# Two decode-attention layers on one core: key and value loads in 16 KB pieces, wq spread over all partitions

## Chip, cores and metric

One Trainium2 chip, one core of it, the other cores idle. The metric is the device time of one execution in microseconds. Every kernel but one was run several times. Where a ratio is given, it is the mean time of one kernel's fast runs over that of the other's fast runs of the same rounds on the same chip, so it is not quite the ratio of the medians that stand beside it.

## The reference

Two independent single-token attention layers, A and B, with the same shapes. A sees only the last 2,048 cache rows, B all 8,192. Everything is bfloat16.

```
x: (1,1,576)   wq: (576, 32*128)   wo: (32*128, 576)   k_cache, v_cache: (1, 16, 8192, 128)
q = (x @ wq) as 32 heads of 128;  two query heads share one of 16 key/value heads
scores = q . k * 128**-0.5 over the window;  p = softmax(scores);  o = p . v
out = concat(o of all heads) @ wo;   A and B are concatenated
```

Nearly all the work is reading. A's keys and values are 16.8 MB, B's 67.1 MB, the two wq 9.4 MB and the two wo 9.4 MB, together 102.8 MB, and every byte is used once.

## The kernel before

A recorder gives every operation an engine and derives the semaphore waits. All large loads go out on one queue (SyncE) into a ring of twelve slots of 1 MB, 8 KB in each of 128 partitions. A slot is loaded again as soon as its last reader is done.

```python
SLOT = 4096; NSLOT = 12                     # bf16 elements per partition and slot; slots

def load_x(P):                              # x as one row
    act.dma_start(xrow[0:1, P * DM:(P + 1) * DM], xs[P][0, 0:1, :])

def load_wq(P, k):                          # five row tiles; the last has only 64 rows = 64 partitions
    rows = 128 if k < 4 else DM - 512
    return load(lambda: wqs[P][k * 128:k * 128 + rows, :], lambda v: v[0:rows, :], "wq")

def load_kv(arrs, P, c, i):                 # B: one head, 32 rows per partition, 8 KB in one run
    ...                                     # A: two heads, 16 rows per partition each, runs of 4 KB
    if HPS[P] == 1:
        return a[0, i, r0:r0 + n, :].rearrange("(p t) d -> p (t d)", p=128)
    return a[0, i * HPS[P]:(i + 1) * HPS[P], r0:r0 + n, :].rearrange("g (p t) d -> p g (t d)", p=128)
```

For each key slot TensorE makes 32 transposes of 128x128 into PSUM, ScalarE and VectorE copy them out, and 8 matmuls of 512 columns build the scores. Each value slot takes 32 matmuls. B's second pass over its keys is mixed with the values of the first, A's values with B's first keys. At the end come B's last 16 value slots and then B's wo, in pieces of 7, 7, 7, 7 and 4 rows per partition, so that the last piece is small.

## Time and profile before

| | before |
|---|---|
| time, median | 263.5 us (263.2 to 264.5) |
| bytes read | 102.8 MB |
| rate while B's 8 KB pieces stream | 420 GB/s |
| rate while A's 4 KB pieces stream | 409 GB/s |
| rate while a 64-row wq piece passes | 248 to 266 GB/s |
| packets on the load queue | 16,328 |

First the busy shares, the DMA rows and the packet count from the page of the kernel before. The two rows cut the span into 40 slices of 6.5 us: the busy share of the DMA engines in tenths, and what they moved.

```profile
PE 171.7 (66%) x3292; PEld 132.6 (51%) x3292; DVE 68.9 (26%) x126; ACT 85.2 (33%) x92; POOL 21.6 (8%) x31
...
DMA  7999999999999999999999999999999999999971
GB/s 263 420 328 409 409 417 419 233 421 414 418 414 410 421 413 414 416 420 416 424 420 419 419 420 421 419 420 420 421 422 415 425 421 419 422 417 421 423 325 55
DMA packets 16369, 103.22 MB, mean 396 GB/s; under 512 B 1618, under 2 KB 1620, under 8 KB 6996
```

The DMA engines are busy from the first load to the last, and no compute engine is above 66%. So a busy digit tells nothing more here; the rate does. Apart from both ends, two slices are low, the third (328) and the eighth (233), and the digit in both is still 9: the engines were occupied, but moved less.

The stretches view of the same kernel puts numbers on these places. After each stretch and its length come the busy times of the five engines, and at the end of the line the granted TensorE clock, the DMA share and the rate.

```profile
core 0: us, PE busy (x) PEld busy (x) DVE busy (x) ACT busy (x) POOL busy (x), PEclk, DMA share, GB/s
12.00:16.00 4.00, 1.04 (x8) 0.14 (x8) 0.00 (x0) 0.00 (x0) 4.00 (x1) 1.00 1.00 266
20.00:36.00 16.00, 15.85 (x238) 12.98 (x237) 8.30 (x12) 11.66 (x13) 2.79 (x9) 1.00 1.03 409
45.00:52.00 7.00, 1.66 (x16) 0.26 (x16) 0.00 (x0) 0.00 (x0) 0.00 (x0) 0.64 1.02 248
110.00:200.00 90.00, 64.94 (x1292) 52.28 (x1289) 31.28 (x53) 38.03 (x41) 0.00 (x0) 0.89 1.01 420
200.00:235.00 35.00, 16.26 (x484) 12.60 (x484) 0.76 (x4) 0.00 (x0) 0.00 (x0) 0.55 1.01 420
```

A missing 154 GB/s over 4 us and a missing 172 GB/s over 7 us, against 420, are 1.5 and 2.9 us of loading. Both stretches are those in which the 64-row tile of a wq passes.

The load queue's own waits, in total us, times, and longest:

```profile
SPq L105 <- PE ktps L335: 13.9, 11, 4.1
SPq L105 <- PE misc L483: 4.4, 4, 2.7
```

The queue (SP is SyncE, ktps the tile of transposed keys) sometimes has to wait for a slot, but none of these waits shows as a gap in the DMA row: twelve slots are far enough ahead.

Last, the end of the kernel, matmuls of wo in order of time (start, duration, instruction, and what was waited for):

```profile
256.08 1.03 PE L483 MATMUL misc<-slots,opj 128*32 128x144 bf16 x28 [1.84 <-DMA slots<-in_B_wo_dram]
257.48 0.67 PE L483 MATMUL misc<-slots,opj 128*32 128x144 bf16 x16 [0.36 <-DMA slots<-in_B_wo_dram]
```

Each piece is used as soon as it lands. What remains after the last landing is 0.7 us of matmuls, a copy and the store.

### The profile page before, as it was taken

The page shows a single profiled execution, that of the slowest core. Times are in us where ns is not written, and L with a number is a line of the kernel's source. Part 1 is how long each engine was busy: PE and PEld are TensorE (multiplying, and loading weights), DVE is VectorE, ACT ScalarE, POOL GpSimd, SP SyncE. Part 2 cuts the span into 40 slices and gives each one's busy share as a digit, 9 for nine tenths or more (in the row PEclk, how much of TensorE's full clock was granted, in tenths as well). Part 3 has the DMA queues.
Part 4 walks back from the last instruction along what each step waited for, and adds up shares of the span by engine and source line. Part 5 has one row for each costly group of instructions (what it writes and reads, how often), then busy time and mean ns, then how long its engine had stood idle before and what let it go on. Part 6 is the DMA issues. An engine that isn't in the chain of part 4 may idle for free.

```text
span 260.6 us, 7123 instructions
## 1 busy us (share of the span) xinstructions
PE 171.7 (66%) x3292; PEld 132.6 (51%) x3292; DVE 68.9 (26%) x126; ACT 85.2 (33%) x92; POOL 21.6 (8%) x31
## 2 busy tenths in 40 slices
PE   0559995179899795778967649768665443443472
PEld 0129781067687564748855438647553333232361
DVE  0014642026345242243633322232244000000000
ACT  2016872036377352445744324333340000000000
POOL 8994000000000000000000000000000000000000
PEclk9999999658799799797999997797886755555555
DMA  7999999999999999999999999999999999999971
GB/s 263 420 328 409 409 417 419 233 421 414 418 414 410 421 413 414 416 420 416 424 420 419 419 420 421 419 420 420 421 422 415 425 421 419 422 417 421 423 325 55
DMA packets 16369, 103.22 MB, mean 396 GB/s; under 512 B 1618, under 2 KB 1620, under 8 KB 6996
## 3 DMA queue, kind: packets, MB, share of 16 engines
q1 hardware_dynamic: 16328, 102.77, 97.4%
q8 instruction: 26, 0.43, 0.7%
q14 instruction: 3, 0.02, 0.0%
q10 hardware_dynamic: 12, 0.00, 0.0%
HBM read 102.76 MB, written 0.00 MB: 394 GB/s over the span
## 4 chain that ended last, share of the span: by engine, by line
DMA 56%; SPq 27%; PE 14%; issue 1%; DVE 1%; ACT 0%
SPq L244 27%; DMA slots<-in_B_v_cache_dram 21%; DMA slots<-in_B_k_cache_dram 10%; DMA slots<-in_B_wo_dram 10%; PE ktps L335 10%; DMA slots<-in_B_wq_dram 9%; DMA slots<-in_A_k_cache_dram 6%; PE sacc L356 2%; PE opsum L448 1%; PE misc L483 0%; DVE qrow L307 0%; PE opsum L298 0%; SPq L105 0%; PE misc L298 0%; DVE srow L411 0%
## 5 line engine op out<-in xcount | busy, mean ns | idle before, releaser
L335 PE MATMUL ktps<-ident,slots 128*128 128x128 bf16 x1280 | 94.0, 243 | 24.6 <-DMA slots<-in_B_k_cache_dram 24.2
L335 PEld LDWEIGHTS ktps<-ident,slots 128*128 128x128 bf16 x1280 | 87.6, 111 | 32.7 <-DMA slots<-in_B_k_cache_dram 28.4
L342 ACT ACTIVATE kt<-ktps 128x1024 bf16<-128x1024 bf16 x80 | 78.7, 1022 | 74.9 <-PE ktps L335 74.8
L345 DVE COPY kt<-ktps 128x1024 bf16<-128x1024 bf16 x80 | 55.4, 692 | 93.0 <-PE ktps L335 93.0
L448 PE MATMUL opsum<-slots,ptm 128*32 128x128 bf16 x1280 | 31.7, 256 | 26.6 <-DMA slots<-in_B_v_cache_dram 26.5
L448 PEld LDWEIGHTS opsum<-slots,ptm 128*32 128x32 bf16 x1280 | 24.5, 114 | 39.7 <-DMA slots<-in_B_v_cache_dram 35.1
L356 PE MATMUL sacc<-kt,qtm 128*32 128x512 bf16 x320 | 25.4, 395 | 0.7 <-DVE kt L345 0.7
L298 PE MATMUL opsum<-slots,xpad 128*32 128x512 bf16 (+1 forms) x40 | 5.6, 542 | 13.0 <-DMA slots<-in_B_wq_dram 7.9
L220 POOL MEMSET ptm<- 128x8192 uint32 x2 | 13.8, 6924 | 0.0
L483 PE MATMUL misc<-slots,opj 128*32 128x144 bf16 x256 | 8.4, 307 | 5.4 <-DMA slots<-in_B_wo_dram 3.3
L461 DVE TENSOR_SCALAR acc<-opsum,stat 128x128 f32<-128x128 f32 x2 | 0.7, 346 | 40.2 <-PE opsum L448 40.2
L298 PEld LDWEIGHTS opsum<-slots,xpad 128*32 128x32 bf16 (+1 forms) x40 | 1.2, 102 | 18.1 <-DMA slots<-in_B_wq_dram 9.9
L483 PEld LDWEIGHTS misc<-slots,opj 128*32 128x32 bf16 x256 | 6.6, 134 | 6.9 <-DMA slots<-in_B_wo_dram 4.2
L305 ACT ACTIVATE qrow<-opsum 128x512 bf16<-128x512 f32 x2 | 1.2, 597 | 25.8 <-PE misc L298 25.8
L356 PEld LDWEIGHTS sacc<-kt,qtm 128*32 128x32 bf16 x320 | 5.0, 95 | 5.9 <-ACT kt L342 1.6
L307 DVE CAST qrow<-misc 128x512 bf16<-128x512 f32 x2 | 1.4, 692 | 20.9 <-PE misc L298 20.9
L298 PE MATMUL misc<-slots,xpad 128*32 128x512 bf16 (+1 forms) x40 | 5.7, 557 | 0.0
L279 PE MATMUL misc<-onesb,xrow 1*128 1x1 bf16 (+1 forms) x10 | 0.8, 171 | 7.4 <-DMA xrow<-in_A_x_dram 7.4
L470 PE MATMUL misc<-acc,pick 128*128 128x32 f32 x16 | 3.5, 380 | 2.7 <-DVE acc L461 1.8
L376 ACT ACTIVATE psb<-sacc,stat 128x1024 bf16<-128x1024 f32 (+1 forms) x3 | 2.9, 971 | 6.8 <-DVE stat L374 6.8
L470 PEld LDWEIGHTS misc<-acc,pick 128*128 128x128 f32 x16 | 3.2, 300 | 3.5 <-DVE acc L461 2.3
L279 PEld LDWEIGHTS misc<-onesb,xrow 1*128 1x128 bf16 (+1 forms) x10 | 0.6, 100 | 7.9 <-DMA xrow<-in_A_x_dram 7.4
(52 smaller groups left out, 34.5 us busy)
## 6 DMA issues: line engine op xcount, KB each, us to landing
slots<-in_B_k_cache_dram SPq DMA_DIRECT2D x32, 1024.0 KB, 26.1
slots<-in_B_v_cache_dram SPq DMA_DIRECT2D x32, 1024.0 KB, 26.9
slots<-in_A_k_cache_dram SPq DMA_DIRECT2D x8, 1024.0 KB, 20.5
slots<-in_A_v_cache_dram SPq DMA_DIRECT2D x8, 1024.0 KB, 22.7
slots<-in_A_wq_dram SPq DMA_DIRECT2D x4, 1024.0 KB, 8.0
slots<-in_B_wq_dram SPq DMA_DIRECT2D x4, 1024.0 KB, 21.1
slots<-in_A_wo_dram SPq DMA_DIRECT2D x4, 1008.0 KB, 27.6
slots<-in_B_wo_dram SPq DMA_DIRECT2D x4, 1008.0 KB, 27.7
```

The source lines that it names most:

```text
L220: add("pool", lambda pool, b=b: pool.memset(ptm[:, b, :].bitcast(U32), 0), writes=[("ptm", b)])
L244: add("sp", lambda sp: sp.dma_start(view_of(slots[:, s, :]), src_of()), writes=[res], dma="slot%d" % s)
L279: ins = pe.matmul(misc[0:n, k:k + 1], lhsT=xrow[0:1, P * DM + k * 128:P * DM + k * 128 + n], rhs=onesb[0:1, 0:1], start=True, stop=True)
L298: ins = pe.matmul(qps[c][32 * j:32 * j + 32, :], lhsT=xpad[0:rows, P, k, :], rhs=slots[0:rows, s, n * 512:(n + 1) * 512], start=(k == 0), ...
L335: ins = pe.matmul(ktps_bf[q][:, t * 128:(t + 1) * 128], lhsT=slots[:, s, (8 * q + t) * 128:(8 * q + t + 1) * 128], rhs=ident[:, :], start= ...
L342: add("act", lambda act, q=q, dst=dst: act.activation(dst, ktps_bf[q], ACT.Copy), reads=[("bank", q)], writes=[("kt", u, q)])
L345: add("dve", lambda dve, q=q, dst=dst: dve.tensor_copy(dst, ktps_bf[q]), reads=[("bank", q)], writes=[("kt", u, q)])
L356: ins = pe.matmul(sacc[32 * j:32 * j + 32, h * 512:(h + 1) * 512], lhsT=qtm[:, P, g * 32:(g + 1) * 32], rhs=kt[:, u, o:o + 512], start=(g ...
L376: add("act", lambda act: act.activation(psb[:, pb, 0:w], sacc[:, 0:w], ACT.Exp, bias=st(P, C_NB + c), scale=SCALE, accum_out=st(P, C_L + c ...
L448: ins = pe.matmul(opsum[32 * j:32 * j + 32, 0:DH], lhsT=ptm[:, pb, o:o + 32], rhs=slots[:, s, t * 128:(t + 1) * 128], start=(g == 0 and b ...
L470: ins = pe.matmul(misc[:, 0:32], lhsT=pick[:, r, :], rhs=acc[:, d, 32 * r:32 * r + 32], start=(r == 0), stop=(r == 3))
L483: ins = pe.matmul(misc[32 * j:32 * j + 32, 0:OUTW], lhsT=opj[:, P, jj:jj + 32], rhs=slots[:, s, o:o + OUTW], start=(jj == 0), stop=(jj == ...
```

## The change

The intent is to have every large load move 16 KB per partition in one contiguous run, over all 128 partitions. Rows of a cache are 256 B, so 16 KB are 64 rows. One head's 2,048 or 4,096 rows then fill only 32 or 64 partitions, and the change fills the others with further heads: partition 4p+g (A) or 2p+g (B) holds rows of head g. wq is read as 64 x 2 runs of 36 KB, in pieces of 16, 16 and 4 KB; wo goes out in pieces of 15.75 and 4.5 KB.

```diff
-SLOT = 4096
-NSLOT = 12
-XT = 5
-WO_SLOT = 7
+SLOT = 8192
+UNIT = 4096
+NSLOT = 6
+TS = 64
+WQ_UNITS = 9
+WQ_SLOT = 4
+WO_SLOT = 14
@@ loads
-        rows = 128 if k < 4 else DM - 512
-        return load(lambda: wqs[P][k * 128:k * 128 + rows, :], lambda v: v[0:rows, :], "wq")
+        lo, hi = k * WQ_SLOT * 2048, min(WQ_UNITS, (k + 1) * WQ_SLOT) * 2048
+        return load(lambda: wqs[P].rearrange("(m r) n -> m (r n)", m=64)
+                    .rearrange("m (e y) -> (m e) y", e=2)[:, lo:hi],
+                    lambda v: v[:, 0:hi - lo], "wq")
-            if HPS[P] == 1:
-                return a[0, i, r0:r0 + n, :].rearrange("(p t) d -> p (t d)", p=128)
-            return a[0, i * HPS[P]:(i + 1) * HPS[P], r0:r0 + n, :].rearrange("g (p t) d -> p g (t d)", p=128)
+            return a[0, i * G[P]:(i + 1) * G[P], r0:r0 + CH[P], :].rearrange("g (p t) d -> p g (t d)", t=TS)
@@ x: one value per (row group, parity), multiplied by a parity mask, instead of a transposed row
+            add("dve", lambda dve, e=e: dve.tensor_scalar(xpad[:, P, 5 * e:5 * e + 5, 0], xtwo[:, P, 0:5],
+                                                          par[2][:, e:e + 1], None, ALU.mult), ...)
@@ scores: every second or fourth column of the transposed keys belongs to a head
-                                        lhsT=qtm[:, P, g * 32:(g + 1) * 32], rhs=kt[:, u, o:o + 512],
+                    rhs = kt[:, u, j * 1024:(j + 1) * 1024].rearrange("d (x g) -> d x g", g=G[P])[:, :, e]
@@ softmax: each probability is written once per interleaved head, then masked by partition
+            src = bass.AP(tensor=sacc, offset=0, ap=[[1024, 128], [1, w], [0, G[P]]])
+                    ins = dve.tensor_scalar(dst, src, par[G[P]][:, e:e + 1], None, ALU.mult)
... (value matmuls, schedule and output store follow the new slots: six of 2 MB)
```

The bytes and the number of key transposes and value matmuls stay the same. About half as many load instructions go out (52 instead of 100).

More of the change, by code (lines that the diff above doesn't have):

```diff
@@ L155, in bass_concat_heads__sliding_block_cached__gqa_block_cached__decode_kernel @@
     base = [SK - W_A, 0]
-    CH = [W_A, SLOT]
-    HPS = [SLOT // CH[P] for P in range(2)]
+    G = [4, 2]
+    PH = [128 // G[P] for P in range(2)]
+    CH = [TS * PH[P] for P in range(2)]
     NCH = [S_len[P] // CH[P] for P in range(2)]
-    NT = [CH[P] // 128 for P in range(2)]
-    CB = [NT[P] // 4 for P in range(2)]
-    CW = [CB[P] * 128 for P in range(2)]
+    UW = [8 * PH[P] for P in range(2)]
+    CW = [2 * UW[P] for P in range(2)]
+    NS = [HKV // G[P] for P in range(2)]
     prog = Program(nc)
@@ L167, in bass_concat_heads__sliding_block_cached__gqa_block_cached__decode_kernel @@
     slots = nc.alloc_sbuf_tensor("slots", [128, NSLOT, SLOT], BF16)
-    kt = nc.alloc_sbuf_tensor("kt", [128, NKT, SLOT], BF16)
+    kt = nc.alloc_sbuf_tensor("kt", [128, NKT, UNIT], BF16)
     ptm = nc.alloc_sbuf_tensor("ptm", [128, 2, 32 * 512], BF16)
-    psb = nc.alloc_sbuf_tensor("psb", [128, 2, 1024], BF16)
+    psb = nc.alloc_sbuf_tensor("psb", [128, 2048], BF16)
     ident = nc.alloc_sbuf_tensor("ident", [128, 128], BF16)
@@ L175, in bass_concat_heads__sliding_block_cached__gqa_block_cached__decode_kernel @@
     selq = nc.alloc_sbuf_tensor("selq", [128, 4], BF16)
-    onesb = nc.alloc_sbuf_tensor("onesb", [128, 4], BF16)
     onesf = nc.alloc_sbuf_tensor("onesf", [128, 4], F32)
     qtm = nc.alloc_sbuf_tensor("qtm", [128, 2, HKV * 32], BF16)
-    xrow = nc.alloc_sbuf_tensor("xrow", [1, 2 * DM], BF16)
-    xpad = nc.alloc_sbuf_tensor("xpad", [128, 2, XT, 32], BF16)
+    xtwo = nc.alloc_sbuf_tensor("xtwo", [128, 2, 8], BF16)
+    xpad = nc.alloc_sbuf_tensor("xpad", [128, 2, 10, 32], BF16)
+    par = [None, None, nc.alloc_sbuf_tensor("par2", [128, 2], F32), None, nc.alloc_sbuf_tensor("par4", [128, 4], F32)]
     qrow = nc.alloc_sbuf_tensor("qrow", [128, 1024], BF16)
@@ L205, in setup @@
         zero(selq[:])
-        pool.memset(onesb[:], 1.0)
         pool.memset(onesf[:], 1.0)
@@ L209, in setup @@
         return zero(qtm[:])
-    add("pool", setup, writes=["ident", "xpad", "selq", "ones", "warm", ("qtm", 0), ("qtm", 1)])
+    add("pool", setup, writes=["ident", ("xpad", 0), ("xpad", 1), "selq", "ones", "warm", ("qtm", 0), ("qtm", 1)])
     def select(t, base_, pattern, mult):
@@ L233, in bass_concat_heads__sliding_block_cached__gqa_block_cached__decode_kernel @@
         add("pool", select(same[:], 32 * dj, [[-1, 128]], 1), reads=["same"], writes=["same"])
+    for n in (2, 4):
+        add("dve", lambda dve, n=n: dve.tensor_reduce(par[n][:, :], ident[:, :].rearrange("p (m g) -> p g m", g=n),
+                                                      AX.X, ALU.add),
+            reads=["ident"], writes=[("par", n)])
     add("act", lambda act: act.activation(warm[:, 4:8], warm[:, 0:4], ACT.Exp), reads=["warm"], writes=["warm2"])
@@ L247, in load_x, with go @@
     def load_x(P):
-        add("act", lambda act: act.dma_start(xrow[0:1, P * DM:(P + 1) * DM], xs[P][0, 0:1, :]),
-            writes=[("xrow", P)], dma="x%d" % P)
+        def go(act):
+            x = xs[P]
+            with nc.allow_non_contiguous_dma(reason="small x load"):
+                src = bass.AP(tensor=x.tensor, offset=x.offset, ap=[[9, 64], [4, 2], [1, 5]])
+                return act.dma_start(xtwo[:, P, 0:5], src)
+        add("act", go, writes=[("xtwo", P)], dma="x%d" % P)
     def load_wq(P, k):
-        rows = 128 if k < 4 else DM - 512
-        return load(lambda: wqs[P][k * 128:k * 128 + rows, :], lambda v: v[0:rows, :], "wq")
+        lo, hi = k * WQ_SLOT * 2048, min(WQ_UNITS, (k + 1) * WQ_SLOT) * 2048
+        return load(lambda: wqs[P].rearrange("(m r) n -> m (r n)", m=64)
+                    .rearrange("m (e y) -> (m e) y", e=2)[:, lo:hi],
+                    lambda v: v[:, 0:hi - lo], "wq")
     def load_kv(arrs, P, c, i):
-        n = CH[P]
-        r0 = base[P] + c * n
+        r0 = base[P] + c * CH[P]
         def src():
             a = arrs[P]
-            if HPS[P] == 1:
-                return a[0, i, r0:r0 + n, :].rearrange("(p t) d -> p (t d)", p=128)
-            return a[0, i * HPS[P]:(i + 1) * HPS[P], r0:r0 + n, :].rearrange("g (p t) d -> p g (t d)", p=128)
-        def view(v):
-            return v if HPS[P] == 1 else v.rearrange("p (g x) -> p g x", g=HPS[P])
-        return load(src, view, "kv")
+            return a[0, i * G[P]:(i + 1) * G[P], r0:r0 + CH[P], :].rearrange("g (p t) d -> p g (t d)", t=TS)
+        return load(src, lambda v: v, "kv")
     def load_wo(P, k):
@@ L275, in x_columns @@
     def x_columns(P):
-        def tr(pe):
-            for k in range(XT):
-                n = 128 if k < 4 else DM - 512
-                ins = pe.matmul(misc[0:n, k:k + 1], lhsT=xrow[0:1, P * DM + k * 128:P * DM + k * 128 + n],
-                                rhs=onesb[0:1, 0:1], start=True, stop=True)
-            return ins
-        add("pe", tr, reads=[("xrow", P), "ones"], writes=[B_M])
-        add("dve", lambda dve: dve.tensor_copy(xpad[:, P, 0:4, 0], misc[:, 0:4]),
-            reads=[B_M], writes=["xpad"])
-        add("dve", lambda dve: dve.tensor_copy(xpad[0:DM - 512, P, 4, 0:1], misc[0:DM - 512, 4:5]),
-            reads=[B_M], writes=["xpad"])
+        for e in range(2):
+            add("dve", lambda dve, e=e: dve.tensor_scalar(xpad[:, P, 5 * e:5 * e + 5, 0], xtwo[:, P, 0:5],
+                                                          par[2][:, e:e + 1], None, ALU.mult),
+                reads=[("xtwo", P), ("par", 2)], writes=[("xpad", P)])
     qps = [opsum, misc]
@@ L291, in q_part @@
     def q_part(P, k, s):
-        rows = 128 if k < 4 else DM - 512
         def mm(pe):
-            for c in range(2):
-                for j in range(4):
-                    n = 2 * j + c
-                    ins = pe.matmul(qps[c][32 * j:32 * j + 32, :], lhsT=xpad[0:rows, P, k, :],
-                                    rhs=slots[0:rows, s, n * 512:(n + 1) * 512],
-                                    start=(k == 0), stop=(k == XT - 1))
+            for u in range(k * WQ_SLOT, min(WQ_UNITS, (k + 1) * WQ_SLOT)):
+                for c in range(2):
+                    for j in range(4):
+                        n = 2 * j + c
+                        x = u // 2 if n // 4 == u % 2 else 5 + (u + 1) // 2
+                        o = (u - k * WQ_SLOT) * 2048 + (n % 4) * 512
+                        ins = pe.matmul(qps[c][32 * j:32 * j + 32, :], lhsT=xpad[:, P, x, :],
+                                        rhs=slots[:, s, o:o + 512], start=(u == 0), stop=(u == WQ_UNITS - 1))
             return ins
-        add("pe", mm, reads=["xpad", ("slot", s)], writes=qbank)
+        add("pe", mm, reads=[("xpad", P), ("slot", s)], writes=qbank)
     def q_finish(P):
@@ L327, in bass_concat_heads__sliding_block_cached__gqa_block_cached__decode_kernel, with k_transpose @@
     k_count = [0]
-    def k_transpose(s):
+    def k_transpose(s, half):
         u = k_count[0] % NKT
@@ L334, in tr @@
                 for t in range(8):
-                    ins = pe.matmul(ktps_bf[q][:, t * 128:(t + 1) * 128],
-                                    lhsT=slots[:, s, (8 * q + t) * 128:(8 * q + t + 1) * 128],
+                    o = (32 * half + 8 * q + t) * 128
+                    ins = pe.matmul(ktps_bf[q][:, t * 128:(t + 1) * 128], lhsT=slots[:, s, o:o + 128],
                                     rhs=ident[:, :], start=True, stop=True, is_transpose=True)
@@ L347, in k_transpose, with k_scores @@
         return u
-    def k_scores(P, i, u):
+    def k_scores(P, i, half, u):
+        w = UW[P]
+        o = half * w
         def mm(pe):
-            for e in range(HPS[P]):
-                g = i * HPS[P] + e
-                for h in range(CW[P] // 512):
-                    for j in range(4):
-                        o = e * CH[P] + j * CW[P] + h * 512
-                        ins = pe.matmul(sacc[32 * j:32 * j + 32, h * 512:(h + 1) * 512],
-                                        lhsT=qtm[:, P, g * 32:(g + 1) * 32], rhs=kt[:, u, o:o + 512],
-                                        start=(g == 0), stop=(g == HKV - 1))
+            for e in range(G[P]):
+                g = i * G[P] + e
+                for j in range(4):
+                    rhs = kt[:, u, j * 1024:(j + 1) * 1024].rearrange("d (x g) -> d x g", g=G[P])[:, :, e]
+                    ins = pe.matmul(sacc[32 * j:32 * j + 32, o:o + w], lhsT=qtm[:, P, g * 32:(g + 1) * 32],
+                                    rhs=rhs, start=(g == 0 and o % 512 == 0), stop=(g == HKV - 1), skip_group_check=True)
             return ins
-        add("pe", mm, reads=[("qtm", P)] + [("kt", u, q) for q in range(4)], writes=B_S[:CW[P] // 512])
+        add("pe", mm, reads=[("qtm", P)] + [("kt", u, q) for q in range(4)], writes=[B_S[o // 512]])
     C_M, C_NB, C_L, C_W, C_AL, C_T = 0, 2, 4, 6, 8, 10
@@ L375, in softmax_exp, with go @@
             reads=[("st", P, C_M + c)], writes=[("st", P, C_NB + c)])
-        add("act", lambda act: act.activation(psb[:, pb, 0:w], sacc[:, 0:w], ACT.Exp, bias=st(P, C_NB + c),
-                                              scale=SCALE, accum_out=st(P, C_L + c)),
-            reads=banks + [("st", P, C_NB + c)], writes=[("psb", pb), ("st", P, C_L + c)])
+        def go(act):
+            src = bass.AP(tensor=sacc, offset=0, ap=[[1024, 128], [1, w], [0, G[P]]])
+            return act.activation(psb[:, 0:w * G[P]].rearrange("p (x g) -> p x g", g=G[P]), src, ACT.Exp,
+                                  bias=st(P, C_NB + c), scale=SCALE, accum_out=st(P, C_L + c))
@@ L379, in softmax_exp @@
+        add("act", go, reads=banks + [("st", P, C_NB + c)], writes=["psb", ("st", P, C_L + c)])
         return pb
     def softmax_transpose(P, c, pb):
-        def tr(pe):
-            for b in range(CB[P]):
-                ins = pe.matmul(misc_bf[:, b * 128:(b + 1) * 128], lhsT=psb[:, pb, b * 128:(b + 1) * 128],
-                                rhs=ident[:, :], start=True, stop=True, is_transpose=True)
-            return ins
-        add("pe", tr, reads=[("psb", pb), "ident"], writes=[B_M])
@@ L389, in put, with tr @@
-        def put(dve):
-            n = CB[P] * 4 * HKV
-            dst = bass.AP(tensor=ptm, offset=pb * 32 * 512 + 30, ap=[[2 * 32 * 512, 128], [32, n], [1, 2]])
-            return dve.tensor_copy(dst, misc_bf[:, 0:2 * n].rearrange("p (n e) -> p n e", e=2))
-        add("dve", put, reads=[B_M], writes=[("ptm", pb)])
+        for u in range(2):
+            def tr(pe, u=u):
+                for t in range(8):
+                    o = (8 * u + t) * 128
+                    ins = pe.matmul(misc_bf[:, t * 128:(t + 1) * 128], lhsT=psb[:, o:o + 128], rhs=ident[:, :],
+                                    start=True, stop=True, is_transpose=True)
+                return ins
+            add("pe", tr, reads=["psb", "ident"], writes=[B_M])
+            n = 32 * NS[P]
+            def put(dve, u=u):
+                for e in range(G[P]):
+                    dst = bass.AP(tensor=ptm, offset=(pb * 32 * 512 + u * n * 32 + 32 - 2 * G[P] + 2 * e),
+                                  ap=[[2 * 32 * 512, 128], [32, n], [1, 2]])
+                    src = misc_bf[:, 0:1024].rearrange("p (n y) -> p n y", y=2 * G[P])[:, :, 2 * e:2 * e + 2]
+                    ins = dve.tensor_scalar(dst, src, par[G[P]][:, e:e + 1], None, ALU.mult)
+                return ins
+            add("dve", put, reads=[B_M, ("par", G[P])], writes=[("ptm", pb)])
@@ L433, in weights @@
             reads=[B_M], writes=[("st", P, C_T + 4)])
-        add("dve", lambda dve: dve.tensor_scalar(st(P, C_AL, n), st(P, C_W, n), st(P, C_T + 4), None, ALU.mult),
+        add("dve", lambda dve: dve.tensor_scalar(st(P, C_AL, n), st(P, C_W, n), st(P, C_T + 4), float(G[P]), ALU.mult,
+                                                  ALU.mult),
             reads=[("st", P, C_T + 4), ("st", P, C_W)], writes=[("st", P, C_AL)])
@@ L441, in mm @@
         def mm(pe):
-            for e in range(HPS[P]):
-                g = i * HPS[P] + e
-                for b in range(CB[P]):
+            for u in range(2):
+                for t in range(8):
                     for j in range(4):
-                        t = e * NT[P] + j * CB[P] + b
-                        o = (b * 4 + j) * 512 + 30 * g + 30
+                        b = 32 * u + 8 * j + t
+                        o = (u * 32 + t * 4 + j) * NS[P] * 32 + (32 - 2 * G[P]) * (i + 1)
                         ins = pe.matmul(opsum[32 * j:32 * j + 32, 0:DH], lhsT=ptm[:, pb, o:o + 32],
-                                        rhs=slots[:, s, t * 128:(t + 1) * 128],
-                                        start=(g == 0 and b == 0), stop=(g == HKV - 1 and b == CB[P] - 1))
+                                        rhs=slots[:, s, b * 128:(b + 1) * 128],
+                                        start=(i == 0 and u == 0 and t == 0),
+                                        stop=(i == NS[P] - 1 and u == 1 and t == 7))
             return ins
@@ L489, in finish_out, with store_out @@
         add("dve", lambda dve: dve.tensor_copy(outsb[:, P, :], misc[:, 0:OUTW]), reads=[B_M], writes=[("outsb", P)])
+    def store_out(P):
         def put(eng):
@@ L494, in put @@
             return eng.dma_start(dst, src)
-        add("act" if P == 0 else "sp", put, reads=[("outsb", P)], writes=[("out", P)], dma="out%d" % P)
+        add("sp", put, reads=[("outsb", P)], writes=[("out", P)], dma="out%d" % P)
     load_x(0)
@@ L501, in k_phase @@
     def k_phase(P, c, between):
-        nslot = HKV // HPS[P]
         pend = None
-        for i in range(nslot):
+        for i in range(NS[P]):
             s = load_kv(ks, P, c, i)
-            u = k_transpose(s)
-            if pend is not None:
-                k_scores(P, *pend)
-            pend = (i, u)
+            for half in range(2):
+                u = k_transpose(s, half)
+                if pend is not None:
+                    k_scores(P, *pend)
+                pend = (i, half, u)
             between(i)
@@ L515, in q_phase @@
         x_columns(P)
-        for k in range(XT):
+        for k in range(3):
             q_part(P, k, load_wq(P, k))
@@ L527, in bass_concat_heads__sliding_block_cached__gqa_block_cached__decode_kernel @@
     q_phase(1)
-    va = list(range(HKV // HPS[0]))
+    va = list(range(NS[0]))
     def between_b0(i):
+        if i == 0:
+            softmax_transpose(0, 0, pa)
         if i == 1:
-            softmax_transpose(0, 0, pa)
-        if i == 2:
             weights(0)
-        if i >= 3 and (i % 3 != 1):
+        if i in (2, 4, 6):
             v_some(0, 0, va, 1)
     pb0 = k_phase(1, 0, between_b0)
-    v_some(0, 0, va, 8)
+    v_some(0, 0, va, NS[0])
     combine(0)
-    vb0 = list(range(HKV))
+    n = 64 * NS[0]
+    stale = ptm[:, 0, 0:32 * n].rearrange("p (n y) -> p n y", y=32)[:, :, 32 - 2 * G[0]:32 - 2 * G[1]]
+    add("pool", lambda pool: pool.memset(stale.bitcast(U32), 0), writes=[("ptm", 0)])
+    vb0 = list(range(NS[1]))
     def between_b1(i):
-        if i == 1:
+        if i == 0:
             softmax_transpose(1, 0, pb0)
-        if i >= 2:
+        if i >= 1:
             v_some(1, 0, vb0, 1)
     pb1 = k_phase(1, 1, between_b1)
-    v_some(1, 0, vb0, HKV)
+    v_some(1, 0, vb0, NS[1])
     v_keep(1, 0)
@@ L553, in bass_concat_heads__sliding_block_cached__gqa_block_cached__decode_kernel @@
     weights(1)
-    for k in range(5):
+    for k in range(3):
         wo_part(0, k, load_wo(0, k))
     finish_out(0)
-    vb1 = list(range(HKV))
-    v_some(1, 1, vb1, HKV)
+    vb1 = list(range(NS[1]))
+    v_some(1, 1, vb1, NS[1])
+    store_out(0)
     combine(1)
-    for k in range(5):
+    for k in range(3):
         wo_part(1, k, load_wo(1, k))
     finish_out(1)
+    store_out(1)
     add("sp", lambda sp: sp.nop(), reads=[("out", 0), ("out", 1)])
```

## The prediction

Where a cut is marked, a passage is gone: the reason given for the slow 64-row pieces, and the one given for its danger. 263.5 - 4.3 - 2.7 - 0.4 + 0.6 comes to 256.7 us, put there as about 256.5.

> **What bounds the kernel now.** Loads. The page counts 102.8 MB, and the sixteen DMA engines are busy in nearly every slice at about 420 GB/s; PE is 66% busy, ACT 33%, DVE 26%. The queue's own waits on compute (13.9 us on the transposes) leave no hole in the DMA row: twelve slots of lookahead cover them. Read by stretches: 409 GB/s while A's keys stream in 4 KB pieces (20 to 36 us), 420 and 421 while B's caches stream in 8 KB pieces (110 to 200 and 200 to 250 us). Three places run slow. From 12 to 16 us the rate is 266 GB/s and from 45 to 52 us 248 GB/s: there the last, 64-row piece of each wq passes, and its 8 KB packets take about 620 to 640 ns instead of 312. The third is the end, 251 to 257 us, where the engines run dry at different times; the change doesn't mend that.
>
> **What the change does, costed.**
> 1. wq over all 128 partitions. At 420 GB/s the two slow stretches would be 1.5 and 2.9 us shorter: about -4.3 us. [...] wo already loads with a 36 KB pitch at full rate (8,064 B in 307 ns), so wq should too.
> 2. 16 KB pieces. Median packets are 160 ns at 4 KB and 312 ns at 8 KB, so, as an estimate, 8 ns each plus 152 ns per 4 KB: 616 ns at 16 KB, 425 GB/s. Packets overlap slightly, so part of the 8 ns may be hidden already. B's 67 MB: -1 to -2.3 us; A's 16.8 MB: -0.7 to -1.6 us.
> 3. Half as many DMAs, so half of the 1,604 completion packets (10 ns each, 100 per engine): -0.4 us.
> 4. Added compute: exp writes each value 2 or 4 times (2,048 columns; 1.1 us now, about 2.1 after), 16 transposes per softmax instead of 4 or 8, masked DVE copies (2.5 us instead of 0.6 to 1.0), A's scores as 128 matmuls of 256 columns instead of 64 of 512. Six 2 MB slots still hold some 24 us of loads, so all this hides, except at the end: the last full wo slot has 56 matmuls instead of 28 (1.03 us per 28 at the halved clock), and the next piece lands 1.4 us later. +0.6 us.
>
> All DMA terms lie on the critical path, because DMA never idles.
>
> **Prediction.** 263.5 - 4.3 - 2.7 - 0.4 + 0.6 is about 256.5 us. Range 252.5 to 262.5. Faster by over 2%: 0.66; within 2%: 0.22; slower: 0.12.
>
> **What would show it.** 16 KB packets at about 616 ns; no slice near 15 and 48 us under 390 GB/s; 423 to 427 GB/s in B's stretches; longer softmax without DMA holes.
>
> **What would make it wrong.** The key and value loads now have a source of 64x2 (or 32x4) rows against 128 partitions. [...]packets would double as the 64-row ones do[...]. Or 16 KB may bring nothing over 8 KB (about 258.5), or coarse slots may let DMA run dry.

## The result

The changed kernel takes 254.8 us (254.6 to 255.1) against 263.5 us, ratio 0.966 (95% interval 0.964 to 0.969). It is correct. A second measurement, told below, gave 0.968.

The page of the changed kernel, lines as above:

```profile
PE 167.1 (66%) x3438; PEld 131.7 (52%) x3438; DVE 79.3 (31%) x141; ACT 87.3 (35%) x92; POOL 22.4 (9%) x31
...
DMA  7999999999999999999999999999999999999960
GB/s 283 398 440 430 433 415 428 433 417 425 432 423 423 430 423 423 433 421 423 430 417 436 425 415 436 430 412 441 421 421 419 430 425 425 428 423 429 425 284 31
DMA packets 7822, 103.24 MB, mean 408 GB/s; under 512 B 1136, under 2 KB 1136, under 8 KB 1648
```

The stretches view of the changed kernel:

```profile
12.00:16.00 4.00, 0.00 (x0) 0.00 (x0) 4.00 (x2) 0.00 (x0) 4.00 (x1) 1.00 0.98 406
20.00:36.00 16.00, 15.15 (x242) 10.40 (x235) 6.53 (x11) 8.25 (x9) 3.06 (x9) 1.00 1.00 426
45.00:52.00 7.00, 5.65 (x102) 3.45 (x102) 2.50 (x6) 4.00 (x4) 0.00 (x0) 1.00 0.99 422
110.00:200.00 90.00, 64.35 (x1320) 52.85 (x1324) 30.49 (x57) 35.75 (x37) 0.53 (x1) 0.85 1.01 425
200.00:235.00 35.00, 12.53 (x463) 10.83 (x456) 0.31 (x1) 0.00 (x0) 0.00 (x0) 0.55 1.01 427
```

Both dips are gone, and everywhere else the rate went from 409 or 420 to about 426 GB/s. The number of packets fell by half. The packet records of the traces give the duration of one packet; medians in ns:

| packet | 4 KB | 8 KB | 16 KB |
|---|---|---|---|
| before | 161 | 312 | |
| after | 159 | | 613 |

The load queue's waits look quite different:

```profile
SPq L108 <- PE ktps L339: 120.7, 20, 10.5
SPq L108 <- PE opsum L464: 36.7, 17, 5.1
...
SPq L108 <- PE misc L302: 25.0, 4, 17.6
```

The queue now waits 120 us for transposes where it waited 14. By itself this means little: with six large slots the next load is refused until a whole 2 MB slot has been read, while the other slots' loads are still under way. The DMA row shows no gap, so the waits cost nothing here. They do tell that the reserve is smaller in steps, and the 17.6 us wait asks for a look. It is for the q matmuls at the start. The timeline of the changed kernel there:

```profile
3.12 13.79 POOL L224 MEMSET ptm<- 128x8192 uint32 x2
...
11.81 6.04 DVE L287 TENSOR_SCALAR xpad<-xtwo,par 128x5 bf16<-128x5 bf16 x2 [8.28 <-DMA xtwo<-in_A_x_dram]
...
18.00 0.62 PE L302 MATMUL opsum<-slots,xpad 128*32 128x512 bf16 x4 [18.00 <-DVE xpad L287]
```

Two multiplies of five elements per partition last 6.0 us, until 17.85 us, and the first q matmul starts at 18.0 us. In the kernel before it started at 8.25 us:

```profile
8.25 0.62 PE L298 MATMUL opsum<-slots,xpad 128*32 128x512 bf16 x4 [0.40 <-DVE xpad L285]
```

Part of the 9.7 us lies before the multiplies: x itself, loaded in a new strided pattern, lands at 11.8 us instead of 7.4 us. The prediction did not see this coming. Whether it costs anything is one of the questions below.

And the end:

```profile
247.95 2.35 PE L500 MATMUL misc<-slots,opj 128*32 128x144 bf16 x72 [2.64 <-DMA slots<-in_B_wo_dram]
```

The 56 matmuls of the last full piece and the 16 of the small one now run as one group. They end at 250.3 us; the last load reports its landing at 249.3 us (its last data packet ends at 248.9 us), so about 1 us remains after the last landing instead of 0.7.

In both kernels the rate falls to about half some 5 us before the last load lands (before: 210 and 218 GB/s at 252 to 254 us; after: 194 and 171 GB/s at 244 to 246 us). Of the sixteen landings of the changed kernel's last load, eight are in by 244.1 us and eight come between 247.4 and 249.3 us. The spread grows on the way: the sixteen landings of one load lie 0.5 us apart at 29 us and 6.5 us at the end. The cause was not looked for.

### The profile page after: what moved, and what is told of

Its sections match the earlier page's. It is cut to its first block, busy times and chain, and to the rows that moved or that the text cites. A ratio compares the mean times of both kernels' runs of the same rounds, so it can differ in the third digit from the quotient of the medians.

```text
span 252.8 us, 7319 instructions
## 1 busy us (share of the span) xinstructions
PE 167.1 (66%) x3438; PEld 131.7 (52%) x3438; DVE 79.3 (31%) x141; ACT 87.3 (35%) x92; POOL 22.4 (9%) x31
## 4 chain that ended last, share of the span: by engine, by line
DMA 53%; PE 38%; DVE 6%; issue 1%; POOL 1%; ACT 0%; SPq 0%; POOLq 0%
DMA slots<-in_B_k_cache_dram 21%; PE ktps L339 20%; DMA slots<-in_B_v_cache_dram 17%; DMA slots<-in_B_wo_dram 11%; PE sacc L362 7%; DMA xtwo<-in_A_x_dram 4%; PE opsum L464 3%; DVE xpad L287 3%; PE opsum L302 2%; PE misc L302 2%; PE misc L500 2%; DVE ptm L407 1%; PE misc L396 1%; PE misc L444 1%; PE misc L431 0%
## 5 line engine op out<-in xcount | busy, mean ns | idle before, releaser
L339 PE MATMUL ktps<-ident,slots 128*128 128x128 bf16 x1280 | 86.4, 231 | 19.1 <-DMA slots<-in_B_k_cache_dram 19.1
L339 PEld LDWEIGHTS ktps<-ident,slots 128*128 128x128 bf16 x1280 | 80.0, 105 | 31.5 <-DMA slots<-in_B_k_cache_dram 20.3
L464 PE MATMUL opsum<-slots,ptm 128*32 128x128 bf16 x1280 | 28.3, 256 | 29.4 <-DMA slots<-in_B_v_cache_dram 28.9
L362 PE MATMUL sacc<-kt,qtm 128*32 128x512 bf16 (+1 forms) x384 | 30.1, 411 | 0.3 <-DVE kt L348 0.3
L302 PE MATMUL opsum<-slots,xpad 128*32 128x512 bf16 x72 | 8.7, 460 | 19.3 <-DVE xpad L287 19.3
L287 DVE TENSOR_SCALAR xpad<-xtwo,par 128x5 bf16<-128x5 bf16 x4 | 6.4, 3098 | 8.3 <-DMA xtwo<-in_A_x_dram 8.3
L302 PE MATMUL misc<-slots,xpad 128*32 128x512 bf16 x72 | 8.5, 450 | 0.0
L385 ACT ACTIVATE psb<-sacc,stat 128x2048 bf16<-128x2048 f32 x3 | 5.9, 1967 | 7.5 <-DVE stat L379 7.5
L407 DVE TENSOR_SCALAR ptm<-misc,par 128x256 bf16<-128x256 bf16 (+1 forms) x16 | 6.9, 526 | 3.7 <-PE misc L396 3.7
L396 PE MATMUL misc<-ident,psb 128*128 128x128 bf16 x48 | 4.1, 235 | 3.7 <-DVE ptm L407 3.7
```

What stands on the lines that cost most here:

```text
L287: add("dve", lambda dve, e=e: dve.tensor_scalar(xpad[:, P, 5 * e:5 * e + 5, 0], xtwo[:, P, 0:5], par[2][:, e:e + 1], None, ALU.mult), read ...
L302: ins = pe.matmul(qps[c][32 * j:32 * j + 32, :], lhsT=xpad[:, P, x, :], rhs=slots[:, s, o:o + 512], start=(u == 0), stop=(u == WQ_UNITS - 1))
L339: ins = pe.matmul(ktps_bf[q][:, t * 128:(t + 1) * 128], lhsT=slots[:, s, o:o + 128], rhs=ident[:, :], start=True, stop=True, is_transpose= ...
L362: ins = pe.matmul(sacc[32 * j:32 * j + 32, o:o + w], lhsT=qtm[:, P, g * 32:(g + 1) * 32], rhs=rhs, start=(g == 0 and o % 512 == 0), stop=( ...
L385: return act.activation(psb[:, 0:w * G[P]].rearrange("p (x g) -> p x g", g=G[P]), src, ACT.Exp, bias=st(P, C_NB + c), scale=SCALE, accum_o ...
L396: ins = pe.matmul(misc_bf[:, t * 128:(t + 1) * 128], lhsT=psb[:, o:o + 128], rhs=ident[:, :], start=True, stop=True, is_transpose=True)
```

## The experiments

The theory has three parts. (A) The 64-row wq tiles run at about half rate (266 and 248 GB/s against 420 in the stretches where they pass), and repairing that is worth about 4.3 us. (B) Every packet costs some 8 ns beyond its bytes (an estimate from the 160 ns at 4 KB and 312 ns at 8 KB), and fewer, larger packets give the rest. (C) All added compute, the late q phase included, hides behind the loads. The rivals: all of the gain comes from one part; or it is the number of DMAs and completions that counts, not the packet size; or the new dealing of rows to partitions matters by itself; or the late start costs time. Twelve runs were made, one of them the changed kernel again. They came in three groups, each on one chip with its own runs of the kernel before (medians 262.9, 263.3 and 263.2 us). The changed kernel ran beside the third group only, so a difference from it in the first two groups compares ratios that were taken on different chips.

### Only the new wq

```diff
 # kernel before, with the changed kernel's x, masks and q matmuls, and:
-        return load(lambda: wqs[P][k * 128:k * 128 + rows, :], lambda v: v[0:rows, :], "wq")
+        return load(lambda: wqs[P].rearrange("(m r) n -> m (r n)", m=64)
+                    .rearrange("m (e y) -> (m e) y", e=2)[:, lo:hi], ...)   # WQ_SLOT = 2: 8 KB pieces
```

> The kernel before with only the new wq and x loads (36 KB pitch over all 128 partitions, cut here into 8 KB pieces so that piece size does not change); keys and values as before. Theory A (the 64-row wq pieces ran at half rate, and that alone is worth about 4.3 us): 259 to 259.6 us, the stretches near 13 and 48 us back at about 420 GB/s, no 8 KB packets near 640 ns. Rival (those slow stretches come from something else, such as the change from wq to key loads or instruction fetches): 263 us, dips still there.

Measured: 258.8 us, ratio 0.984 (0.982 to 0.986), so 4.2 us (1.58% of 263). Its stretches view:

```profile
12.00:16.00 4.00, 0.00 (x0) 0.00 (x0) 4.00 (x2) 0.00 (x0) 4.00 (x1) 1.00 1.01 410
45.00:52.00 7.00, 4.76 (x93) 2.76 (x90) 2.09 (x7) 1.38 (x3) 0.00 (x0) 1.00 1.02 425
110.00:200.00 90.00, 67.27 (x1308) 54.09 (x1309) 30.34 (x53) 36.24 (x39) 0.00 (x0) 0.83 1.01 420
```

The dips are gone and the rate in B's part is what it was. In the packet records, 99 of 100 of the 8 KB packets are now at or under 326 ns; in the kernel before that mark lay at 640 ns. Part A holds, in place and in size.

### Only the large pieces

```diff
 # changed kernel, with the old x and wq: two 8 KB row tiles per 2 MB slot, each its own DMA,
 # the fifth over 64 partitions
+            for k in ks_:
+                rows = 128 if k < 4 else DM - 512
+                out_.append(sp.dma_start(slots[0:rows, s, (k % 2) * 4096:(k % 2) * 4096 + 4096],
+                                         wqs[P][k * 128:k * 128 + rows, :]))
```

By the theory wq's 4.3 us are missing here and the rest of the gain stays. The expectation is cut where it named a cause for the 4.3 us.

> The changed kernel with the old wq and x loads (five row tiles, the last over 64 partitions, in 8 KB pieces). Theory A+B ([...]piece size and fewer DMAs about 3.5 to 4.5): 258.5 to 260 us with both dips back. If the gain were all piece size: about 255; if all of it were wq: about 263.

Measured: 259.5 us, ratio 0.987 (0.985 to 0.989), so 3.5 us, give or take 0.6. This kernel also has the larger wo pieces and the longer tail of the changed one. Its stretches view shows the dips back and the faster stream kept:

```profile
12.00:16.00 4.00, 1.97 (x20) 0.53 (x24) 0.00 (x0) 0.00 (x0) 4.00 (x1) 1.00 1.07 295
45.00:52.00 7.00, 4.53 (x61) 1.51 (x53) 1.03 (x5) 2.06 (x2) 0.00 (x0) 0.82 0.99 242
110.00:200.00 90.00, 64.99 (x1316) 51.10 (x1308) 32.81 (x57) 37.69 (x40) 0.53 (x1) 0.86 1.01 425
```

The two parts are separate and nearly add up: 1.58% and 1.33% against 3.2 to 3.4% for the whole. Of the remaining 0.3 to 0.5% (about 1 us), wq's own larger pieces, which neither kernel has, account for some 0.3 us as an estimate (32 packets per engine fewer than the new wq in 8 KB pieces, at 9 ns); the rest is of the size of the intervals.

### The same slots in smaller pieces

Layout, compute and waits of the changed kernel stay; only the number of pieces per slot changes.

```diff
-        return load(src, lambda v: v, "kv")
+        W_ = SLOT // 2            # or SLOT // 4
+        def go(sp):
+            return [sp.dma_start(slots[:, s, h * W_:(h + 1) * W_], src()[:, :, h * W_:(h + 1) * W_])
+                    for h in range(2)]         # or range(4)
+        add("sp", go, writes=[("slot", s)], dma="slot%d" % s, n_dma=2)
```

> The changed kernel, each 2 MB key or value slot loaded by two DMAs of 8 KB pieces; layout, compute and waits the same. Theory B (each packet costs about 8 ns beyond its bytes): 320 more packets per engine are 2.6 us, 40 more completion packets 0.4 us, so about 257.8 us and about 420 GB/s. Rival (piece size is nothing above 8 KB; the interleaved rows or wq gave the gain): at most 255.3.

Measured: 257.6 us, ratio 0.980 (0.978 to 0.982).

> The same with four DMAs of 4 KB pieces. Theory B, linear in the number of packets: 960 more packets and 120 more completions per engine, 7.7 + 1.2 us, about 263.7 us and about 410 GB/s. Rival (no cost per packet): 255 to 256.

Measured: 263.4 us, ratio 1.002 (1.000 to 1.004): with 4 KB pieces for all keys and values the whole gain of the change is gone, although wq's repair is still in it (B's pieces are then smaller than the 8 KB of the kernel before).

The two stretches of B's part, of the kernel with two pieces and then of that with four:

```profile
110.00:200.00 90.00, 64.85 (x1288) 52.72 (x1288) 31.59 (x58) 36.00 (x38) 0.53 (x1) 0.83 1.01 420
```

```profile
110.00:200.00 90.00, 63.74 (x1303) 51.09 (x1301) 31.31 (x50) 37.29 (x38) 0.53 (x1) 0.86 1.03 410
```

So 410, 420 and 425 GB/s for 4, 8 and 16 KB with one and the same layout. With the ratios, and 0.967 (the mean of the two measurements) for the changed kernel: two pieces cost 1.3% or 3.4 us for 320 more packets per engine, four cost 3.5% or 9.2 us for 960. That is 10.6 ns per added packet, give or take 2, and 9.5 ns, give or take 0.7, with the added completions in it. The packet records of the load queue alone, between 110 and 200 us, give 407.8, 417.9 and 423.4 GB/s for 4, 8 and 16 KB (the view counts the other queues too), or about 8 ns per added packet as an estimate. The rival that interleaving by itself matters falls too: at 8 KB the interleaved layout streams at 420 GB/s, like the plain one of the kernel before.

### More DMAs, same pieces

Two pieces per slot also mean twice the DMAs. To separate the two, each head got its own DMA, into every second or fourth partition, still 16 KB at a time.

```diff
+            return [sp.dma_start(slots[g:128:G[P], s, :],
+                                 a[0, i * G[P] + g, r0:r0 + CH[P], :].rearrange("(p t) d -> p (t d)", t=TS))
+                    for g in range(G[P])]
```

> The changed kernel, each 2 MB key or value slot loaded by one DMA per head (every second or fourth partition), so 16 KB pieces, the same layout, but 56 more DMAs and completion packets per engine. Theory (bytes per packet count, the number of DMAs hardly): 56 completions of 10 ns, +0.6 us, about 255 us, ratio to before 0.968 to 0.971. Rival (splitting into 2 x 8 KB lost 3 us because of its 40 extra DMAs): 56 extra DMAs lose about 4.5 us, 258.5 to 259 us, ratio 0.983.

Measured: 254.7 us, ratio 0.968 (0.966 to 0.971). Its stretch in B's part:

```profile
110.00:200.00 90.00, 64.57 (x1360) 52.49 (x1355) 31.34 (x57) 35.54 (x37) 0.53 (x1) 0.83 1.01 426
```

56 more DMAs cost about 0.3 us, give or take 0.7. That rules out the rival's 4.5 us, so it was mainly the packet size that cost 3.4 us above. It doesn't tell the 0.6 us of the theory from nothing. The packet records do: between 110 and 200 us the load queue moved 423.5 GB/s here and 423.5 and 423.4 GB/s in the two profiles of the changed kernel, where one more completion of 9 ns (what its record lasts) per slot and engine would have left 422.7 as an estimate. So the added completions cost nothing that can be seen, and the prediction's 0.4 us for fewer of them wasn't found.

### One head per partition half

```diff
+            return [sp.dma_start(slots[64 * g:64 * g + 64, s, :],           # B only; the result is wrong
+                                 a[0, i * 2 + g, r0:r0 + CH[P], :].rearrange("(p t) d -> p (t d)", t=TS))
+                    for g in range(2)]
```

The theory is that 64 neighbouring partitions halve the rate whatever is loaded into them, as with the old wq tile. The cause it gave is cut; no trace of this case shows it.

> Wrong result on purpose. The changed kernel, but each of B's key and value slots is loaded by two DMAs of one head each, one into partitions 0 to 63, one into 64 to 127, 16 KB pieces. Theory ([...]): packets of about 1.2 us in B's phases, about 210 to 300 GB/s there, so 350 to 420 us in all. Rival (the 64-row wq piece was slow for another reason, partition choice is free): about 255 us.

Measured, in one look whose state is unknown: 420.9 us, at the upper edge of what was expected; wrong result, as intended. Its stretch in B's part, against 425 above:

```profile
110.00:200.00 90.00, 44.16 (x718) 35.14 (x717) 19.35 (x30) 23.63 (x24) 0.53 (x1) 0.73 1.00 234
```

The median 16 KB packet took 1,149 ns instead of 613. The run before this one also used 64 partitions per DMA, with the same 16 KB pieces, but every second one, and was at full rate (426 GB/s). So it was not the number of partitions that counted but which: with 64 neighbours the rate was 234 GB/s. The doubled packets look like those of the old wq tile (8 KB in about 620 to 640 ns instead of 312), without wq. Why neighbours are slow the traces do not show.

### The late start of q

```diff
-            add("dve", lambda dve, e=e: dve.tensor_scalar(xpad[:, P, 5 * e:5 * e + 5, 0], xtwo[:, P, 0:5],
-                                                          par[2][:, e:e + 1], None, ALU.mult), ...)
+            add("act", lambda act, e=e: act.activation(xpad[:, P, 5 * e:5 * e + 5, 0], xtwo[:, P, 0:5],
+                                                       ACT.Copy, scale=par[2][:, e:e + 1]), ...)
```

> The changed kernel with the four tiny masked multiplies of x moved from VectorE to ScalarE. In the trace of the changed kernel two of them, 128x5 elements each, last until 17.85 us (6.0 us as a group) while GpSimd clears ptm, and the first q matmul starts at 18.0 us instead of 8.3. Theory (they wait for GpSimd, and loads ahead hide it): first q matmul near 12.3 us, time unchanged within 0.5 us, 254 to 255. Rival (the late start costs time): 2 us or more faster.

Measured: 255.1 us, ratio 0.969 (0.967 to 0.972), no gain. Its timeline:

```profile
12.05 0.50 ACT L287 ACTIVATE xpad<-xtwo,par 128x5 bf16<-128x5 bf16 x2 [9.31 <-DMA xtwo<-in_A_x_dram]
...
12.69 0.62 PE L302 MATMUL opsum<-slots,xpad 128*32 128x512 bf16 x4 [12.69 <-ACT xpad L287]
```

The multiplies take 0.5 us on ScalarE while GpSimd still clears ptm, and q starts 5.3 us earlier, for nothing: the delay was hidden. (The other 4.4 us against the kernel before come with the later landing of x.) That it was GpSimd that held VectorE up is read from the traces, as no run took the memsets away. The tile's view of the changed kernel has all four multiplies; after the count stand the shortest, median and longest duration in ns:

```profile
L287 DVE TENSOR_SCALAR xpad<-xtwo,par x4: 228/3066/6031, 11.8 to 49.6; 128x5 bf16<-128x5 bf16 x4
```

Layer B's two, at 49.4 us with GpSimd idle, take 0.23 us each. Layer A's two take 5.9 and 6.0 us. In all nine traces with these multiplies on VectorE, layer A's begin anywhere between 9.6 us (only the new wq) and 12.6 us (one DMA per head) and yet end between 17.83 and 17.86 us, just after GpSimd's last memset there (17.80 to 17.82 us). In the changed kernel they last from 11.8 to 17.85 us, past the end of the long memsets at 16.9 us and through the shorter ones queued behind them (the last ended at 17.8 us): as far as this profile's rough GpSimd spans allow, it was a run of GpSimd instructions that held them up, not just one. They did not hold up every VectorE instruction: in the kernel before, two casts at 7.9 us took 0.17 and 0.14 us while GpSimd cleared ptm. What makes the difference the traces do not show.

How well hidden it was, two runs with fewer slots tell.

```diff
-NSLOT = 6
+NSLOT = 4
```

> The changed kernel with four 2 MB slots instead of six. Theory (the late q phase is hidden only by six slots): the first four loads, 6.8 MB, are in by about 18.5 us, the first slot comes free near 20.6 us and refills about 2 us later, so a hole of about 4 us in the DMA row near 20 us, and 258 to 261 us. If lookahead did not matter: 254.5 us.

Measured: 260.0 us, ratio 0.989 (0.985 to 0.992). The stretches view shows the hole where it was expected:

```profile
16.00:18.00 2.00, 0.01 (x4) 0.04 (x5) 1.84 (x2) 0.00 (x0) 1.85 (x6) 1.00 1.01 434
18.00:20.00 2.00, 2.00 (x20) 0.84 (x24) 0.00 (x0) 0.00 (x0) 1.71 (x4) 1.00 0.29 123
20.00:22.00 2.00, 2.00 (x24) 0.84 (x20) 0.00 (x0) 0.00 (x0) 1.57 (x5) 1.00 0.00 0
22.00:24.00 2.00, 1.91 (x36) 0.79 (x28) 0.04 (x1) 0.04 (x1) 1.43 (x5) 1.00 0.60 197
```

> Four 2 MB slots, with the masked multiplies of x on ScalarE. With four slots alone the DMA row had a hole of about 4.5 us at 18 to 24 us and the time was 260.0 us (ratio 0.989). Theory (the hole comes from the late q phase, itself from VectorE waiting for GpSimd): first q matmul near 12.7 us, the first slot free near 16.5 to 17 us, hole gone or under 1 us, 255.5 to 256.5 us, ratio about 0.972. Rival (the hole is a matter of four slots alone): 259 to 260 us.

Measured: 257.5 us, ratio 0.978 (0.976 to 0.981), 1 us more than expected. The first hole is closed, but a weaker stretch from 44 to 58 us is left; its cause was not followed further.

```profile
20.00:22.00 2.00, 2.00 (x40) 2.00 (x38) 1.15 (x4) 1.49 (x2) 1.58 (x4) 1.00 0.99 426
...
44.00:58.00 14.00, 9.56 (x154) 6.08 (x147) 3.80 (x8) 5.86 (x9) 0.00 (x0) 0.88 0.84 324
```

So the late q phase is a real delay that six slots hide and four do not. Part C holds for six slots, and two slots fewer are already too few.

### The yardstick again, and a smaller tail

> The changed kernel unedited, as the yardstick for the other kernels of this call: 254 to 255 us, ratio to before about 0.967.

Measured: 254.8 us, ratio 0.968 (0.966 to 0.970).

```diff
-WO_SLOT = 14                                  # pieces of 14, 14 and 4 rows
+WO_CUT = [[0, 14, 28, 32], [0, 13, 24, 29, 32]]   # B: 13, 11, 5 and 3 rows
```

> The changed kernel with B's wo pieces cut 13, 11, 5 and 3 rows per partition instead of 14, 14 and 4, so that less matrix work is left after the last landing. In the changed kernel 56 plus 16 matmuls run for 2.4 us from the last but one landing, 1 us past the last one. Theory: some 0.5 us less, ratio to before 0.965 against 0.967 for the changed kernel; within noise is possible. Rival (the extra DMA costs as much): equal.

Measured: 254.4 us, ratio 0.967 (0.965 to 0.969) beside 0.968 on the same chip. The median is 0.3 us lower, but the intervals overlap, so no gain is shown. It is correct.

### The next doubling

Pieces of 32 KB (128 rows), 4 or 8 heads interleaved, three slots of 4 MB in the same memory, x on ScalarE, and smaller wo pieces.

```diff
-SLOT = 8192
-NSLOT = 6
-TS = 64
-    G = [4, 2]
+SLOT = 16384
+NSLOT = 3
+TS = 128
+    G = [8, 4]
 ... (four units per slot instead of two, wo in pieces of 16, 9, 5 and 2 rows)
```

> The next doubling: 32 KB pieces, three slots of 4 MB, 4 (B) or 8 (A) heads interleaved over partitions, x on ScalarE, wo in pieces of 16, 9, 5 and 2 rows. The law of 8 ns per packet gives 352 fewer 16 KB packets replaced by half as many of 32 KB, about 1.4 us, and 0.3 us for fewer DMAs: 252.5 to 253.5 us and 428 GB/s, packets of 1,220 ns, if three slots suffice. Rival (three slots with 4 MB steps let the DMA queue run dry, as four 2 MB slots did at the start): holes in the DMA row and 256 to 265 us. I think the rival likelier.

Measured: 329.3 us, ratio 1.25; correct, and far outside what was expected either way. Its DMA rows, slices of 8.2 us, and two stretches, one in which A's keys load and one in B's part:

```profile
DMA  8999999919399999999999995899999409999994
GB/s 320 364 212 196 212 218 270 382 59 400 130 446 447 252 202 229 394 222 222 206 430 426 430 428 234 324 442 446 426 411 416 140 2 352 444 446 414 418 420 177
```

```profile
26.00:46.00 20.00, 9.88 (x142) 7.95 (x143) 4.15 (x6) 5.84 (x6) 0.00 (x0) 0.70 1.01 212
164.00:192.00 28.00, 18.82 (x336) 15.77 (x336) 9.49 (x22) 9.13 (x10) 0.95 (x1) 0.81 1.00 429
```

Two things happen. There are holes (2 GB/s and 59 GB/s in single slices), which the rival had foreseen: the queue waits up to 28.4 us for one slot. But the larger loss, some 47 of the 74.5 us as an estimate (570 packets of over 2,000 ns, each about 1,320 ns longer than B's, over 16 engines), is in slices with a full DMA digit and half the rate. The packet records name them: while A's caches load, the median 32 KB packet takes 2,530 ns, and while B's load it takes 1,213 ns. B deals 32 rows times 4 heads over the partitions, which A did in the changed kernel at full rate (426 GB/s). A now deals 16 rows times 8 heads, and runs at half rate (212 GB/s). That is the danger the prediction named, packets that double as the 64-row ones do; it was not there at 64x2 and 32x4 (613 ns at 16 KB), and is there at 16x8. The doubled packets look like those of 64 neighbouring partitions (1,149 ns at 16 KB), but the traces do not show what doubles them, so the cause stays open. A rival on the reading side was not tested either: a load of A here reads eight heads side by side that lie 2 MB apart in memory, where the loads at full rate read two or four.

B's 32 KB packets fit the law: 159, 309, 611 and 1,213 ns are the most common durations at 4, 8, 16 and 32 KB, which is about 8.4 ns plus 150.6 ns per 4 KB. The next doubling would be worth about 1.4 us by that law, as an estimate, if it did not cost slots and A's dealing.

## Why the prediction was right

It said 256.5 us with 252.5 to 262.5; measured were 254.8 us. Its two main terms, wq and the pieces, were each found by a run of their own. The tail's 0.6 us is too small for the intervals of these runs.

| term | predicted | measured |
|---|---|---|
| wq over all partitions | -4.3 us | -4.2 us (only the new wq) |
| larger pieces, fewer DMAs and tail | -2.7, -0.4 and +0.6, together -2.5 us | -3.5 us (only the large pieces, which has the tail too) |
| of this, tail | +0.6 us | about +0.3 us (1.0 against 0.7 us after the last landing) |
| added compute, otherwise | 0 | no hole in the DMA row (six slots) |
| whole | -7.0 us | -8.7 us (the two runs add to -7.7; for the rest see the second experiment) |

1. What bounds the kernel: right. In the runs above the time follows the bytes per second of the load stream and the holes in it, and with six slots moving compute (x on ScalarE) changed nothing (255.1 us, ratio 0.969).
2. wq: right in place and size. The neighbouring-partition run shows the halved rate without wq in it (234 GB/s instead of 425).
3. Pieces: right in kind, and with completions and tail too small by about 1 us (-2.5 against -3.5 us, give or take 0.6). The estimate of 8 ns per packet was good: with equal layout the rates in B's part give 8 ns, the times 9.5 to 10.6 ns. Two steps made the term small. One is the discount, "Packets overlap slightly, so part of the 8 ns may be hidden already": the DMA share of 1.01 in B's stretch does show some overlap, but no hidden part of the 8 ns was found. The other is that it counted the keys and values alone. Before the change A had 256 and B 512 packets per engine, after it 320 in all; 448 fewer at 9 ns are 4.0 us as an estimate. wo (32 fewer) and wq (24 fewer) add 0.5 us, which the prediction left out.
4. Completions: the run with more DMAs shows no cost of them in the load rate, and none clear of noise in the time, so this term was too large.
5. Compute hides: right for the whole, but the prediction left out the largest piece of it. It costed exp, transposes and masked copies, and not the later landing of x and the two five-element multiplies that together started q 9.7 us later. Here it was lucky: that this cost nothing is the merit of six slots. With four, the multiplies' share of it cost about 2.5 us (260.0 against 257.5 us).
6. The danger it named, doubled packets from the new dealing of rows, did not arise with 64x2 and 32x4 (16 KB in 613 ns). The 16x8 run (32 KB in 2,530 ns instead of 1,213) suggests that it was one step away.

## What to carry to other kernels

When a kernel only streams, look at the rate in each stretch and not at the busy share: a full DMA digit with a low rate was here a load into 64 neighbouring partitions (234 GB/s), or one in small pieces (409 or 410 GB/s at 4 KB), or A's 16x8 dealing (212 GB/s). Count packets as well as bytes; here some 9 ns per packet made 4, 8 and 16 KB pieces differ by 2.2% and 1.3% of the whole. Before doubling again, check with one run that the new dealing of rows to partitions still runs at full rate and that the ring still has enough slots: bigger pieces cost reserve, and here the reserve was what hid the late q phase (254.8 us with six slots, 260.0 us with four).
